# Decayed attention, routed experts and a Mish layer: attention scores on two row halves, updates by heads, counting one step later, and six experts taken in falling order of their counts

## The chip, the core and the metric

The program runs on one core of a Trainium2 chip. Its engines are TensorE (PE; PEld is its weight load), VectorE (DVE), ScalarE (ACT), GpSimd (POOL) and SyncE (SP), each with a queue of its own that it works through in order; DMA queues move data between the device memory and the two on-chip memories, SBUF and PSUM. The metric is device time in microseconds; smaller is better.

## What is computed

Three stages, one behind the other, all in float32. Attention with a decay by blocks (2 batches, 8 heads, 768 rows, 64 per head); a layer of 8 experts, where each of the 1536 rows goes to the one expert of its largest logit; and a dense layer with a Mish curve.

```
for b in range(nb):                                   # blocks of the sequence
    intra = einsum('bhic,bhjc->bhij', qb, kb) * Dmask    # lam ** (i - j), lower triangle
    intra = einsum('bhij,bhjd->bhid', intra, vb)
    inter = einsum('bhid,bhde->bhie', qb * lam_pow, kv_state)
    out[:, :, sl] = intra + inter
    kv_state = lam_block * kv_state + einsum('bhsd,bhse->bhde', kb * rev_pow, vb)

expert_idx = argmax(x @ w_gate)                       # experts
for e in range(E):
    mask = expert_idx == e
    out[mask] = gate_w[mask, None] * (maximum(x[mask] @ w1[e], 0) @ w2[e])

h = x @ w_in                                          # dense layer
return (h * tanh(log1p(exp(h)))) @ w_out
```

## The kernel before

Attention runs in 12 steps, `STEPS`: 6 chunks of 128 rows for each of 2 batches, in turn. Step i first asks for the tiles of step i + 2 (`load_step`: k_t, q, v_n, k_n; three buffers each, all on SP's queue). Then `scores(i + 1)` multiplies keys and queries; q lies in the tile `qbd`, 2 x 64 rows with zeros in the other half, so that one matmul of 256 columns (line 393) gives both heads of a pair. VectorE multiplies the scores by the decay table `dec` (line 397). `factors(i + 1)` runs on GpSimd: `kd` (line 409), then `qs` in two operations, the sum of the two halves of `qbd` (line 415) and the product with the powers `pw` (line 416). `rows(i - 1)` turns the finished rows and forms the logits (line 474); `pick(i - 1)` finds the largest on VectorE, and its one-hot row goes to `oh_all` (line 501). `values(i)` adds state times q (line 433) and scores times v (line 442, in column halves) in PSUM, and then forms the update `u` of the state (line 451, four matmuls of which half is used). `place(i - 1)`, the counting, comes next: two small matmuls (lines 510 and 511) give each row its slot in its expert's bin, VectorE adds the one-hot rows to `obs` (line 526) and writes `slot_i` (line 527), ScalarE scales the rows by their gate (lines 517 and 521), and GpSimd scatters them to the bins in device memory (line 533). `update(i)` ends the step (line 465). In steps 1 to 8 a piece of expert weights (128 x 1024) is loaded and split in two f32r parts: the high part on ScalarE (line 189), the low part on VectorE one step later (line 194).

The experts' stage takes expert after expert in 4 chunks each, `g` of 32, always with a window of `WIN` = 232 columns. `up(g)` (line 719) has 24 f32r matmuls of 232 columns; `down(g - 1)` (lines 740 and 743) has eight of 464 columns and eight of 232. The weights come in 64 pieces, in the order of the experts; `advance(2 * g + 7)` splits them three chunks ahead. `tables()` works out, on VectorE and before the first chunk, where each expert's rows begin in the result (`off_i`) and which rows lie outside the window. `pad(e)` writes zero rows behind each bin from GpSimd's queue, and `load_x(e)` fetches a bin on SP's queue. The dense layer follows in 48 chunks. At the very end a branch (line 882) runs a slow loop for rows outside the windows, if there are any.

The code is written in the order in which it runs; each engine takes its instructions in that order, and a wait holds everything behind it on the same engine.

Of the kernel before, what the change touches and what calls it, by code (L numbers as in the profile page):

```python
# [11 lines left out]
F32 = mybir.dt.float32  # L12
# [27 lines left out]
REST = WIN - P  # L40
FF = 2048
# [5 lines left out]
NX = -(-NT // WIN) - 1  # L47
# [13 lines left out]
def kernel(  # L61
# [52 lines left out]
    cmax = const.tile([P, NE], F32, name="cmax")  # L114
# [5 lines left out]
    eps = const.tile([P, 1], F32, name="eps")  # L120
# [44 lines left out]
    with tc.manual_schedule():  # L165
# [9 lines left out]

        def load_piece():
# [93 lines left out]
        with ExitStack() as actx:  # L270
            ap = actx.enter_context(pool("attn"))

            qbd = []
            for i in range(3):
                t = ap.tile([P, 2, NP, P], F32, name=f"qbd{i}")
                qbd.append(t)
            DVE.memset(qbd[0][HD:P, 0], 0.0)
            DVE.memset(qbd[0][0:HD, 1], 0.0)
            for t in qbd[1:]:
                POOL.memset(t[0:HD, 1], 0.0)  # L280
                POOL.memset(t[HD:P, 0], 0.0)

# [41 lines left out]

            dec = ap.tile([P, NH, P], F32, name="dec")
            pw = ap.tile([P, NP, P], F32, name="pw")
# [4 lines left out]
            def decay(g):  # L331
                h = slice(4 * g, 4 * g + 4)
                DVE.tensor_copy(out=sc0[:, h, :], in_=lam_b[:, h].unsqueeze(2).to_broadcast([P, 4, P]))
# [5 lines left out]
            def powers():  # L339
                DVE.tensor_copy(out=sc0[:, 0:NP, :], in_=lam_p.unsqueeze(2).to_broadcast([P, NP, P]))  # L340
# [19 lines left out]
            POOL.memset(eps, 1e-9)  # L360
# [5 lines left out]
            def constants():  # L366
                for i, (n, b) in enumerate(STEPS):
                    POOL.iota(tok[:, i:i + 1], pattern=[[0, 1]], base=b * SEQ + n * P, channel_multiplier=1)
                POOL.iota(
                    steps, pattern=[[WIN, NX]], base=WIN, channel_multiplier=0, allow_small_or_imprecise_dtypes=True)  # L370
# [3 lines left out]
                POOL.memset(ones8, 1.0)  # L374
                POOL.memset(zeros, 0.0)
# [3 lines left out]
            pt, qs, kd, xt, sld, rk, us, direct = {}, {}, {}, {}, {}, {}, {}, {}  # L379
            NS = len(STEPS)  # L380

            def scores(i):
# [4 lines left out]
                for g in range(2):  # L387
                    if i == 0:
                        decay(g)
                    a = ps.tile([P, 2, 2 * P], F32, tag="a", name=f"a{i}_{g}", bufs=3)  # L390
                    for j in range(2):
                        hp = 2 * g + j
                        PE.matmul(
                            out=a[:, j, :].rearrange("p (a i) -> p a i", a=2), lhsT=k_t[:, hp, :], rhs=q[:, :, hp, :],
                            start=True, stop=True)
                    t = ap.tile([P, 4, P], F32, tag="pt", name=f"pt{i}_{g}", bufs=4)
                    DVE.tensor_tensor(
                        out=t.rearrange("p h i -> p (h i)"), in0=a.rearrange("p h i -> p (h i)"),
                        in1=dec[:, 4 * g:4 * g + 4, :].rearrange("p h i -> p (h i)"), op=ALU.mult)
                    pt[i, g] = t  # L400

            def factors(i):
# [4 lines left out]
                if n < NCH - 1:  # L407
# [3 lines left out]
                        in1=dec[:, :, P - 1:P].to_broadcast([P, NH, HD]), op=ALU.mult)  # L411
# [15 lines left out]
            def values(i):  # L427
# [10 lines left out]
                for h in range(NH):  # L438
                    if h == NH // 2 and i == NS - 2:
                        place(i - 1)  # L440
# [566 lines left out]
```

## Time and profile before

| | us |
|---|---|
| median of 3 runs | 542.11 (541.70 to 542.39) |
| the profiled execution | 541.75 |
| its span, first to last instruction | 540.1 |
| TensorE busy | 522.6 (97%) |
| VectorE busy | 369.8 (68%) |
| ScalarE busy | 324.7 (60%) |
| GpSimd busy | 185.2 (34%) |

By the trace attention lasts up to about 87 us, the experts up to about 269 us, and the dense layer to the end. The shares are means over the three stages, whose limits differ. An f32 matmul appears as two records in the trace, an f32r or bf16 matmul as one. The duration of a matmul record reaches into the next one; the distance of their starts tells the pace.

### The profile page before, as it was taken

Reading aid. Unit: us, or ns where it says so; the run is one execution under the profiler, and the core shown is the slowest. Engines: PE = TensorE matmul, PEld = TensorE weight load, DVE = VectorE, ACT = ScalarE, POOL = GpSimd, SP = SyncE. Lnnn points to the kernel's source line nnn. Section 1 sums busy time; section 2 is a strip of 40 time slices with the busy share of each in tenths; the row PEclk is TensorE's granted clock in tenths of the full one; section 3 lists DMA queues with packets and bytes.
Section 4 is the critical chain, followed back from the end, with each engine's and each line's share of the span. In section 5 each row is a group of like instructions: output and inputs, shape, how many; then the busy total and the mean of one; then the engine's idle time right before and its main releaser. Section 6 shows DMA issues by size and latency. Waiting matters only on the chain. (4 is left out here: it accounts for less than half of the span.)

```text
span 540.1 us, 8441 instructions
## 1 busy us (share of the span) xinstructions
PE 522.6 (97%) x3101; PEld 451.4 (84%) x3102; DVE 369.8 (68%) x668; ACT 324.7 (60%) x514; POOL 185.2 (34%) x151
## 2 busy tenths in 40 slices
PE   8999988999999999999999999999999999999993
PEld 5888878999999999999788878888888888888882
DVE  7999965765967858653498776567965778436362
ACT  1566533655674566555678876777666775765650
POOL 7788842755573331235100321003210031103032
PEclk9999999999999999999999999999999999999997
DMA  8999837119999996731301024020230000001022
GB/s 259 340 329 332 277 147 292 52 49 399 315 299 224 223 360 236 262 128 40 118 0 62 18 79 133 23 79 0 95 139 4 0 0 1 0 1 58 21 80 81
DMA packets 28944, 74.98 MB, mean 139 GB/s; under 512 B 6652, under 2 KB 6652, under 8 KB 28896
## 3 DMA queue, kind: packets, MB, share of 16 engines
q1 hardware_dynamic: 25040, 66.62, 38.3%
q0 software_dynamic: 3424, 7.23, 3.6%
q8 instruction: 26, 0.43, 0.4%
q10 hardware_dynamic: 432, 0.53, 0.3%
q14 instruction: 22, 0.18, 0.1%
HBM read 66.61 MB, written 10.49 MB: 143 GB/s over the span
## 5 line engine op out<-in xcount | busy, mean ns | idle before, releaser
L194 POOL TENSOR_TENSOR lo_f<-w,hi_f 128x1024 fp32r<-128x1024 f32 x16 | 39.8, 2487 | 185.9 <-ACT hi_f L189 155.1
L719 PE MATMUL h<-x,hi_w 128*128 128x232 f32 x512 | 87.5, 274 | 0.0
L740 PE MATMUL y<-hh,hi_w 128*128 128x464 f32 x256 | 84.8, 380 | 0.9 <-DVE hh L723 0.9
L796 PE MATMUL hp<-yt,hi_f 128*128 128x512 f32 x256 | 79.3, 391 | 0.0
L719 PEld LDWEIGHTS h<-x,hi_w 128*128 128x128 f32 x512 | 77.8, 192 | 0.0
L828 PE MATMUL acc<-hi_f,ghi 128*128 128x512 f32 x192 | 76.2, 397 | 0.4 <-ACT Y L833 0.4
L828 PE MATMUL acc<-hi_f,glo 128*128 128x512 f32 x192 | 75.8, 395 | 0.0
L828 PE MATMUL acc<-lo_f,ghi 128*128 128x512 f32 x192 | 75.7, 394 | 0.0
L136 DVE TENSOR_TENSOR t<-t,hp 128x512 f32<-128x512 f32 x48 | 32.8, 684 | 61.1 <-ACT t L135 61.1
L719 PE MATMUL h<-x,lo_w 128*128 128x232 f32 x256 | 71.1, 278 | 0.0
L743 PE MATMUL y<-hh,lo_w 128*128 128x232 f32 x256 | 69.1, 270 | 0.0
L194 DVE TENSOR_TENSOR lo_w<-raw,hi_w 128x1024 fp32r<-128x1024 f32 x50 | 63.0, 1283 | 7.5 <-ACT hi_w L189 6.9
L132 ACT ACTIVATE t<-hp 128x512 f32<-128x512 f32 x48 | 28.6, 600 | 62.4 <-PE hp L796 62.1
L189 ACT ACTIVATE hi_w<-raw 128x1024 fp32r<-128x1024 f32 x64 | 64.5, 1055 | 0.9 <-DMA raw<-in_w1p_dram 0.9
L194 POOL TENSOR_TENSOR lo_w<-raw,hi_w 128x1024 fp32r<-128x1024 f32 x14 | 35.1, 2510 | 71.5 <-ACT hi_w L189 70.8
L796 PEld LDWEIGHTS hp<-yt,hi_f 128*128 128x128 f32 x256 | 48.1, 188 | 11.1
L740 PEld LDWEIGHTS y<-hh,hi_w 128*128 128x128 f32 x256 | 48.2, 188 | 6.1 <-DVE hh L723 1.1
L796 PE MATMUL hp<-yt,lo_f 128*128 128x512 f32 x128 | 50.4, 394 | 0.0
L719 PEld LDWEIGHTS h<-x,lo_w 128*128 128x128 f32 x256 | 49.0, 191 | 0.5
L743 PEld LDWEIGHTS y<-hh,lo_w 128*128 128x128 f32 x256 | 48.9, 191 | 0.0
L722 ACT ACTIVATE hh<-h 128x464 fp32r<-128x464 f32 x32 | 17.8, 558 | 49.7 <-PE h L719 45.2
L723 DVE SCALAR_TENSOR_TENSOR hh<-h,hh 128x464 fp32r<-128x464 f32 x32 | 20.4, 639 | 34.8 <-ACT hh L722 34.8
(163 smaller groups left out, 1032.9 us busy)
## 6 DMA issues: line engine op xcount, KB each, us to landing
raw<-in_w1p_dram SPq DMA_DIRECT2D x32, 512.0 KB
raw<-in_w2p_dram SPq DMA_DIRECT2D x32, 512.0 KB
w<-in_w3p_dram SPq DMA_DIRECT2D x32, 512.0 KB
xw<-bins SPq DMA_DIRECT2D x7, 512.0 KB
qbd<-in_qT_dram SPq DMA_DIRECT2D x24, 128.0 KB
v_n<-in_vN_dram SPq DMA_DIRECT2D x12, 256.0 KB
k_n<-in_kN_dram SPq DMA_DIRECT2D x10, 256.0 KB
k_t<-in_kT_dram SPq DMA_DIRECT2D x10, 256.0 KB
```

The costliest lines, as they stand in the source:

```text
L132: yield lambda: ACT.activation(out=t, in_=h, func=AF.Tanh, scale=0.5)
L136: yield lambda: DVE.tensor_tensor(out=t, in0=t, in1=h, op=ALU.mult)
L189: ACT.activation(out=hi, in_=r, func=AF.Copy)
L194: engine.tensor_tensor(out=lo, in0=r, in1=hi.bitcast(F32), op=ALU.subtract)
L719: PE.matmul(out=p[:, m, :], lhsT=w[:, s], rhs=x[k // 2][:, k % 2, r, :], start=(k == 0 and m == 0 and z == 0), stop=(k == KD - 1 and z == ...
L722: ACT.activation(out=h[:, :, 0, :], in_=p, func=AF.Relu)
L723: DVE.scalar_tensor_tensor(out=h[:, :, 1, :], in0=p, scalar=0.0, in1=h[:, :, 0, :].bitcast(F32), op0=ALU.max, op1=ALU.subtract)
L740: PE.matmul(out=y.rearrange("p z n -> p (z n)"), lhsT=whi[:, s], rhs=h[:, f].rearrange("p z n -> p (z n)"), start=(c == 0 and f == 0), sto ...
L743: PE.matmul(out=y[:, 1, :], lhsT=wlo[:, s], rhs=h[:, f, 0, :], start=False, stop=(c == 3 and f == 1), skip_group_check=True)
L796: PE.matmul(out=p, lhsT=w[:, s], rhs=x, start=(k == 0 and z == 0), stop=(k == KD - 1 and z == 2))
L828: PE.matmul(out=acc[t], lhsT=x[:, s], rhs=w[:, DM:2 * DM], start=(first and z == 0), stop=(last and z == 2))
```

## The change

Attention. q is loaded as it is, without zeros (one transfer a step in place of two), and the scores are eight matmuls a step on the two halves of the rows, 64 each, that write two PSUM tiles by turns; `dec` is ordered by halves accordingly. `qs` is one operation on GpSimd. The update `u` is eight matmuls by heads, 64 by 64 each. `place` is cut into `weigh`, `locate` and `scatter`: the gate's scaling stays in the step, the counting and the scatter of a row tile come one step later. The negated maximum and the sum for the gate move from VectorE to ScalarE. The split of weight pieces begins in step 3 and not in step 1; 16 pieces are loaded before the experts' stage and not 19.

Experts. Experts 0 and 1 keep their places and 232 columns. The six others are sorted by falling count on the chip; place by place they get windows of 232, 212, 200, 192, 180 and 168 columns. Their weights and rows are fetched by an index that SP reads from the table `who_i`. The loop at the end takes what lies outside the windows in pieces of 128 rows.

```diff
+WINS = (WIN, WIN, 232, 212, 200, 192, 180, 168)
+NSORT = 6
+OWIN = P
...
+        def expert(e):
+            if e not in experts:
+                j = e - (NE - NSORT)
+                experts[e] = SP.value_load(who_i[0:1, j:j + 1], min_val=0, max_val=NE - 1)
+            return experts[e]
...
-            SP.dma_start(out=r, in_=(w1p, w2p)[s][e, c])
+            w = (w1p, w2p)[s]
+            if e < NE - NSORT:
+                SP.dma_start(out=r, in_=w[e, c])
+            else:
+                SP.dma_start(out=r, in_=w[ds(expert(e), 1), c].rearrange("o p f -> p (o f)"))
...
-                q = qbd[i % 3]
+                q = ap.tile([P, NP, P], F32, tag="q", name=f"q{i}", bufs=3)
...
-                SP.dma_start(out=q[0:HD, 0], in_=qT[i, 0:HD])
-                SP.dma_start(out=q[HD:P, 1], in_=qT[i, HD:P])
+                SP.dma_start(out=q, in_=qT[i])
...
+                a = [ps.tile([P, NP, P], F32, tag="a", name=f"a{i}_{z}", bufs=3) for z in range(2)]
+                for hp in range(NP):
+                    for z in range(2):
+                        r = slice(z * HD, (z + 1) * HD)
+                        PE.matmul(out=a[z][:, hp, :], lhsT=k_t[r, hp, :], rhs=q[r, hp, :], start=True, stop=True)
...
-                    POOL.tensor_tensor(out=s, in0=q[:, 0], in1=q[:, 1], op=ALU.add)
-                    POOL.tensor_tensor(out=s, in0=s, in1=pw, op=ALU.mult)
+                    POOL.tensor_tensor(out=s, in0=q, in1=pw, op=ALU.mult)
...
-                    for hp in range(NP):
+                    for h in range(NH):
+                        hp, z = divmod(h, 2)
                         PE.matmul(
-                            out=u[:, hp, :], lhsT=kd[i][:, 2 * hp:2 * hp + 2, :].rearrange("p h d -> p (h d)"),
-                            rhs=v_n[:, hp * P:(hp + 1) * P], start=True, stop=True)
-                if 1 <= i < NS - 2:
-                    place(i - 1)
+                            out=u[z * HD:(z + 1) * HD, hp, :], lhsT=kd[i][:, h, :],
+                            rhs=v_n[:, h * HD:(h + 1) * HD], start=True, stop=True)
...
-                DVE.tensor_scalar(out=nm, in0=m8[:, 0:1], scalar1=-1.0, scalar2=None, op0=ALU.mult)
+                ACT.activation(out=nm, in_=m8[:, 0:1], func=AF.Copy, scale=-1.0)
...
                 scores(i + 1)
+                if 2 <= i < NS - 1:
+                    locate(i - 2)
...
                 factors(i + 1)
+                if 2 <= i < NS - 1:
+                    scatter(i - 2)
...
+                if 1 <= i < NS - 1:
+                    weigh(i - 1)
                 values(i)
...
-                if 1 <= i <= 8:
+                if 3 <= i <= 8:
                     p, r = next_raw()
...
-            for _ in range(5):
+            for _ in range(2):
                 load_piece()
...
         def tables():
...
+            DVE.tensor_tensor(
+                out=above, in0=key[:, n0:NE].unsqueeze(1).to_broadcast([P, NSORT, NSORT]),
+                in1=key[:, n0:NE].unsqueeze(2).to_broadcast([P, NSORT, NSORT]), op=ALU.is_gt)
+            DVE.tensor_reduce(out=rank, in_=above, axis=AX.X, op=ALU.add)
...
+            by_place(who_f, iota8[:, n0:NE])
+            DVE.tensor_copy(out=who_i, in_=who_f)
...
-        with tc.If(flag > WIN):
+        with tc.If(flag > 0):
```

TensorE, one step of attention, before. `a` are the scores, `r` the turned rows with the logits, `o` the values, `u` the update, `c` the counts:

```order
L393 MATMUL a_0_611<-qbd_107,k_t_514 128x256 x2
L393 MATMUL a_1_616<-qbd_107,k_t_514 128x256 x2
L474 MATMUL r_0_631<-rw,xt_575 128x136 x3
L474 MATMUL r_1_632<-rw,xt_575 128x136
L433 MATMUL o_651<-qs_534,state_160 128x128 x4
L442 MATMUL o_651<-pt_0_525,v_n_427 64x128 x4
L442 MATMUL o_651<-pt_1_530,v_n_427 64x128 x4
L451 MATMUL u_666<-v_n_427,kd_532 128x128 x4
L510 LDWEIGHTS tri
L510 MATMUL c_671<-obs,tri 128x8
L511 LDWEIGHTS tri
L511 MATMUL c_671<-oh_all,tri 128x8
```

The same engine after, from the update of one step to the state of the next:

```order
L471 MATMUL u_428<-v_n_196,kd_298 64x64 x8
L414 MATMUL a_0_447<-q_349,k_t_350 128x128
L414 MATMUL a_1_448<-q_349,k_t_350 128x128
...
L540 LDWEIGHTS tri
L540 MATMUL c_461<-obs,tri 128x8
L541 LDWEIGHTS tri
L541 MATMUL c_461<-oh_all,tri 128x8
L492 MATMUL r_0_478<-rw,xt_426 128x136 x3
L492 MATMUL r_1_479<-rw,xt_426 128x136
L454 MATMUL o_503<-qs_380,state_163 128x128 x4
```

The count matmuls stood behind the update of their step; now they stand behind the scores, one step later. The two score tiles alternate, and the update has smaller matmuls.

GpSimd, one step of attention, before (`bins` is the scatter):

```order
L533 DMA bins<-xs_588,slot_i 12288x512
L409 TENSOR_TENSOR kd_621<-k_n_520,dec 128x512
L415 TENSOR_TENSOR qs_623<-qbd_107 128x512
L416 TENSOR_TENSOR qs_623<-qs_623,pw 128x512
L533 DMA bins<-xs_677,slot_i 12288x512
```

And after:

```order
L555 DMA bins<-xs_500,slot_i 12288x512
L431 TENSOR_TENSOR kd_661<-k_n_540,last 128x512
L437 TENSOR_TENSOR qs_663<-q_534,pw 128x512
L555 DMA bins<-xs_596,slot_i 12288x512
L431 TENSOR_TENSOR kd_759<-k_n_638,last 128x512
```

One operation in four is gone; the order of the others is the same, but the scatter belongs to an earlier step.

SP at the start of the experts' stage, after (`xw` are an expert's rows, `raw` its weight pieces):

```order
L760 DMA xw_1323<-bins 128x2x512
L195 TENSOR_LOAD who_i
L195 ISA x2
L208 ISA
L208 DMA raw_1670<-in_w1p_dram 128x1024
L208 ISA
L208 DMA raw_1685<-in_w2p_dram 128x1024
L762 ISA
L762 DMA xw_1691<-bins 128x2x512
L208 ISA
L208 DMA raw_1741<-in_w1p_dram 128x1024
```

Before, three more pieces stood ahead of the first of these `xw` loads and none between the first and the second; now two stand between them, behind the read of `who_i`.

## Rows read from the trace of the kernel before

**Rows 1.** Stretches (us): length, busy time by engine, PEclk, DMA share, GB/s

```profile
12.00:31.00 19.00, 18.10 (x154) 16.34 (x153) 17.86 (x53) 9.25 (x24) 16.12 (x32) 1.00 1.04 340
31.00:69.00 38.00, 36.74 (x297) 30.91 (x296) 35.91 (x108) 23.18 (x60) 32.16 (x24) 1.00 0.97 311
69.00:87.00 18.00, 15.44 (x125) 13.40 (x124) 11.52 (x57) 5.68 (x17) 7.10 (x8) 1.00 0.57 214
87.00:178.00 91.00, 90.09 (x695) 87.06 (x694) 62.18 (x88) 51.25 (x75) 51.64 (x33) 1.00 0.71 228
```

**Rows 2.** Timeline of PE in attention: start, duration, line, output<-inputs, records

```profile
18.63 1.97 PE L393 MATMUL a<-qbd,k_t 128*128 128x256 f32 x8
...
24.41 1.97 PE L393 MATMUL a<-qbd,k_t 128*128 128x256 f32 x8
...
43.22 1.97 PE L393 MATMUL a<-qbd,k_t 128*128 128x256 f32 x8
45.18 1.19 PE L474 MATMUL r<-rw,xt 128*128 128x136 f32 x8
46.21 1.05 PE L433 MATMUL o<-qs,state 128*128 128x128 f32 x8
47.20 1.09 PE L442 MATMUL o<-pt,v_n 128*64 128x128 f32 x16
48.22 1.16 PE L451 MATMUL u<-v_n,kd 128*128 128x128 f32 x8
49.22 0.17 PE L510 MATMUL c<-obs,tri 128*128 128x8 bf16 x1
49.60 0.17 PE L511 MATMUL c<-oh_all,tri 128*128 128x8 bf16 x1 [0.21 <-DVE oh_all L501]
```

**Rows 3.** Timeline of POOL in the same step, and of a later one

```profile
43.10 2.21 POOL L416 TENSOR_TENSOR qs<-qs,pw 128x512 f32<-128x512 f32 x1
46.18 1.01 POOL L533 DMA_INDIRECT bins<-xs,slot_i  x1 [0.86 <-DVE state L465]
47.22 1.06 POOL L409 TENSOR_TENSOR kd<-k_n,dec 128x512 f32<-128x512 f32 x1
48.23 1.27 POOL L415 TENSOR_TENSOR qs<-qbd 128x512 f32<-128x512 f32 x1
...
68.02 1.27 POOL L416 TENSOR_TENSOR qs<-qs,pw 128x512 f32<-128x512 f32 x1
```

**Rows 4.** Timeline of DVE in the same step

```profile
44.50 0.83 DVE L526 TENSOR_TENSOR obs<-obs,oh_all 128x8 bf16<-128x8 bf16 x1
...
48.42 1.12 DVE L501 TENSOR_SCALAR oh_all<-iota,i 128x8 bf16<-128x8 f32 x1
49.46 1.21 DVE L194 TENSOR_TENSOR lo_w<-raw,hi_w 128x1024 fp32r<-128x1024 f32 x1
```

**Rows 5.** Timeline of PEld: first loads of the values, of the update

```profile
47.19 0.20 PEld L442 LDWEIGHTS o<-pt,v_n 128*64 128x64 f32 x4
...
48.22 0.41 PEld L451 LDWEIGHTS u<-v_n,kd 128*128 128x128 f32 x3 [0.17 <-issue]
```

**Rows 6.** Timeline of PE in the experts' stage: end of an up, begin of a down

```profile
119.48 0.28 PE L719 MATMUL h<-x,lo_w 128*128 128x232 f32 x1
...
120.83 0.38 PE L740 MATMUL y<-hh,hi_w 128*128 128x464 f32 x1
121.04 0.27 PE L743 MATMUL y<-hh,lo_w 128*128 128x232 f32 x1
121.14 0.38 PE L740 MATMUL y<-hh,hi_w 128*128 128x464 f32 x1
```

**Rows 7.** Timeline of PE: the last logits, 8 columns each

```profile
79.44 1.06 PE L482 MATMUL lg<-rw,xt 128*128 128x8 f32 x8 [0.70 <-ACT xt L446]
```

**Rows 8.** Timeline of DVE at the start of the experts' stage

```profile
88.47 0.17 DVE L648 TENSOR_TENSOR_SCAN incl<-ones,base 128x8 f32<-128x8 f32 x1
...
90.66 0.17 DVE L664 TENSOR_TENSOR pos_i<-pos_f,slot_f 128x12 int32<-128x12 f32 x1
92.87 1.19 DVE L723 SCALAR_TENSOR_TENSOR hh<-h,hh 128x464 fp32r<-128x464 f32 x2 [2.04 <-ACT hh L722]
```

More of the change, by code (lines that the diff above doesn't have):

```diff
@@ L46 @@
 UNITS = 33
-NX = -(-NT // WIN) - 1
+NX = -(-(NT - min(WINS)) // OWIN)
 NPIECE = NE * 8
@@ L113 @@
     first_i = const.tile([P, NE, NX], I32, name="first_i")
-    cmax = const.tile([P, NE], F32, name="cmax")
+    key = const.tile([P, NE], F32, name="key")
+    above = const.tile([P, NSORT, NSORT], F32, name="above")
+    rank = const.tile([P, NSORT], F32, name="rank")
+    sel = const.tile([P, NSORT, NSORT], F32, name="sel")
+    part = const.tile([P, NSORT, NSORT], F32, name="part")
+    count = const.tile([P, NE], F32, name="count")
+    who_f = const.tile([P, NSORT], F32, name="who_f")
+    who_i = const.tile([P, NSORT], I32, name="who_i")
+    at_f = const.tile([P, NE], F32, name="at_f")
+    wins = const.tile([P, NE], F32, name="wins")
+    thr = const.tile([P, NE], F32, name="thr")
+    over_f = const.tile([P, NE, NX], F32, name="over_f")
+    cmax = const.tile([P, 8], F32, name="cmax")
     cmax_i = const.tile([P, 1], I32, name="cmax_i")
@@ L174 @@
         n_load, n_split = [0], [0]
+        experts = {}
+        def expert(e):
[3 more added lines that the diff above has]
+            return experts[e]
         def load_piece():
@@ L325 @@
             dec = ap.tile([P, NH, P], F32, name="dec")
+            lam_z = lam_b.rearrange("p (h z) -> p z h", z=2)
+            last = ap.tile([P, NH], F32, name="last")
             pw = ap.tile([P, NP, P], F32, name="pw")
@@ L374, in constants @@
                 POOL.memset(ones8, 1.0)
+                for j, w in enumerate(WINS):
+                    POOL.memset(wins[:, j:j + 1], float(w - OWIN))
                 POOL.memset(zeros, 0.0)
@@ L443, in values @@
                         out=o[z * HD:(z + 1) * HD, hp, :], lhsT=v_n[:, h * HD:(h + 1) * HD],
[L444 removed]
+                        rhs=pt[i, z][:, hp, :], start=(n == 0 and hp == 0), stop=True, skip_group_check=True)
                 x = ap.tile([P, NP, P], F32, tag="xt", name=f"xt{i}", bufs=2)
@@ L521, in place, with locate @@
                     ACT.activation(out=xs[:, n:NP], in_=rv[1], func=AF.Copy, scale=gt[:, 0:1])
+            def locate(i):
+                c = ps.tile([P, NE], F32, tag="c", name=f"c{i}", bufs=1)
+                PE.matmul(out=c, lhsT=tri[:, 1, :], rhs=obs, start=True, stop=False)
+                PE.matmul(out=c, lhsT=tri[:, 0, :], rhs=oh_all[:, i, :], start=False, stop=True)
                 jk = ap.tile([P, NE], F32, tag="jk", name=f"jk{i}", bufs=1)
@@ L531, in place, with scatter @@
                         out=hot, in0=iotaw, scalar1=slot_f[:, i:i + 1], scalar2=None, op0=ALU.is_equal)
-                    direct[i] = (xs, hot)
+                    direct[i] = (xg[i], hot)
+            def scatter(i):
                 POOL.indirect_dma_start(
                     out=bin_views[i], out_offset=IOA(ap=slot_i[:, i:i + 1], axis=0),
-                    in_=xs.rearrange("p a c -> p (a c)"), in_offset=None)
+                    in_=xg.pop(i).rearrange("p a c -> p (a c)"), in_offset=None)
+            def place(i):
+                weigh(i)
+                locate(i)
+                scatter(i)
             def spread(i, g, start):
@@ L569 @@
                 late = []
+                if 1 <= i < NS - 1:
+                    weigh(i - 1)
                 values(i)
+                if i == NS - 2:
+                    locate(i - 1)
+                    scatter(i - 1)
                 if i == 0:
@@ L578 @@
                 if i in (9, 10):
-                    for _ in range(2):
+                    for _ in range(3):
                         load_piece()
@@ L736, in down @@
                 for m in range(KD):
-                    y = ys[e][m]
+                    y = ys[e][m][:, :, 0:w]
                     for f in range(2):
                         s = slice(f * DM + m * P, f * DM + (m + 1) * P)
-                        PE.matmul(out=y.rearrange("p z n -> p (z n)"), lhsT=whi[:, s],
-                                  rhs=h[:, f].rearrange("p z n -> p (z n)"), start=(c == 0 and f == 0), stop=False,
+                        PE.matmul(out=y, lhsT=whi[:, s], rhs=h[:, f], start=(c == 0 and f == 0), stop=False,
                                   skip_group_check=True)
@@ L912, in overflow @@
             DVE.tensor_copy(out=xt[:, 2 * g:2 * g + 2, :], in_=p)
-        h = op.tile([P, NE, WIN], F32, name="o_h")
-        y = [ps.tile([P, 2, WIN], F32, tag=f"y{i}", name=f"o_y{i}", bufs=1) for i in range(2)]
+        h = op.tile([P, NE, OWIN], F32, name="o_h")
+        y = [ps.tile([P, 2, OWIN], F32, tag=f"y{i}", name=f"o_y{i}", bufs=1) for i in range(2)]
         for c in range(4):
```

158 lines of the change are left out of this document (84 added, 74 removed).

## The prediction

> **What bounds the kernel now.** I read the stages first [rows 1]. In the experts' stage TensorE works 90.09 of 91 us, so a saving there counts in full, but only if it shortens what TensorE itself does. In attention it also looks full (36.74 of 38 us), yet three others are as full: VectorE 35.91, GpSimd 32.16, and the DMA engines at a share of 0.97 while they move 311 GB/s (1.04 at 340 GB/s in the stretch before). The granted clock is 1.00, the 2.4 GHz level, in all of them; I expect no change of it.
>
> Then one attention step on TensorE [rows 2]. From the scores at 43.22 to the count matmul at 49.60, plus its 0.10, a step is 6.48 us: scores 1.96, r 1.03, state times q 0.99, values o 1.02, update u 1.00, counting 0.48. In the last row TensorE waits 0.21 for the one-hot rows. Steps without the load of a split are shorter: 5.78 from 18.63 to 24.41. An f32 matmul stands as two records: eight records of 256 columns in 1.96 are 0.24 each.
>
> What sets 6.48 is a ring between GpSimd and VectorE. GpSimd's rows fill it [rows 3]: wait 0.86, scatter 1.01, kd 1.06, sum of the q halves 1.27, product with pw 2.21, and small gaps. The scatter needs slot_i, which stands behind the update of obs; that tiny bf16 operation takes 0.83 and ends at 45.33, as GpSimd's product (43.10 before it, 2.21 long) ends at 45.31 [rows 3, 4]. In the same way the one-hot operation takes 1.12 and ends at 49.54, as the sum of the halves ends at 49.50. So two VectorE operations on eight columns, a size that costs 0.17 elsewhere [rows 8], wait for GpSimd to finish, and GpSimd waits for the first of them. The product takes 1.27 where no weight split runs on VectorE (68.02) and 2.21 where one does (49.46, 1.21 long).
>
> **The change part by part.**
>
> *Plain q, scores on row halves.* Removed: GpSimd's sum of the halves (1.27 and 0.09 of gap in each step), the zeroing of the q tiles, one DMA per step. The four score matmuls of 256 columns become eight of 128 columns on 64 rows, in pairs on the two halves. No row of before shows row halves. Column halves do exist there: the values o are 16 records of 128 columns in 1.02, where u needs 1.00 for eight [rows 2], so the two halves run side by side. Their weight loads do too: four loads of 64 columns lie within 0.20, where three of 128 columns lie within 0.41, that is 0.19 and twice 0.11 [rows 5]; four in a row at half of 0.11 would reach 0.30. I take row halves to behave as column halves: eight pairs of records at 0.112, 0.90. The other end is no overlap, 16 times 0.112, 1.79.
>
> *Change of tiling.* The three groups from 46.21 to 49.22 hold two changes and take 3.01 (u's 1.00 included), where 24 slots of 0.111 are 2.66: 0.17 for a change. Before there are two in a step, after there are three (u to scores, scores to count, state to values): 0.52.
>
> *Update by heads.* Four matmuls of 128 by 128 become eight of 64 weight columns and 64 moving columns, in the tiling of the values. Pairs at half of 0.112 give 0.45; if a pair can't go under 0.112, 0.90. I take 0.55, near the low end, since the loads of [rows 5] came at that pace.
>
> *TensorE's new step*: 0.90 + 0.55 + 0.52 + r 0.93 + state 0.90 + o 0.87 + count 0.05 = 4.7; at the bad ends 6.0.
>
> *Counting a step back.* The count matmuls move behind the scores of the next step, so the 0.21 goes. The wait is put on VectorE instead: the reciprocal now follows three ScalarE operations in a row (negated maximum, exponential, weight), with the state update and the next masks queued behind it. With a weight split ahead of it (1.21) that is covered; without one I count 0.5, in steps that VectorE doesn't bound. The scatter moves on GpSimd's queue too, from behind values to behind the factors, and its rows leave one step later.
>
> *The ring after.* GpSimd keeps 6.48 - 1.36 = 5.1; with the product at 1.27, 4.2. VectorE, full today, loses its two small operations (0.3) and up to 1.5 of waiting: 4.7. DMA: a step moves four tiles of 0.26 MB, a weight piece of 0.52 and a scatter of 0.26, 1.83 MB; at 340 GB/s 5.4, at 311 5.9, and q as one transfer over all partitions may be quicker. So the next limit is DMA, hardly above the others. I take 5.4 for the six steps with a split (two fewer pieces are split here than before): six times 1.1, 6.5. The three before them go from 5.8 to 5.0 (4.7 and some of the 0.5), 2.5. The start, without zeroing, gives 0.5. For the last two steps, where TensorE idles 2.56 of 18 [rows 1], I take a step's 1.1 and 0.9 from the shorter product. **Attention: 11.5**, between 3.5 and 15.
>
> *Windows of 232 to 168 columns.* The experts lose 20, 32, 40, 52 and 64 columns, 208 in all. Up: twelve records of 232 columns take 120.83 - 119.48 = 1.35, 0.112 each [rows 6]. Eight records of only 8 columns, with the same 128-column weights, take 1.06 [rows 7]; if the last lasts 0.28 as in [rows 6], they start 0.111 apart. So it is the weight load that sets the pace of up, and fewer columns give nothing there. The Trainium skill, "TensorE: Matmul & The Clock Gate", section Back-to-back issue gap, gives N/2.4 + 2.5 ns for a lone matmul; by that, up would shrink with the columns; the trace has 112 where it gives 99. Down: a pair is one matmul of two times 232 columns, 0.21, and one of 232, 0.10 [rows 6]. The second can't fall (a weight load must fit in it); the first falls by 0.21/464 = 0.453 ns a column, 32 times an expert: 32 x 2 x 208 x 0.453 = **6.0**. Bounds 5.5 and 7.
>
> *Sorting.* Tables on VectorE: 13 operations in 2.36 (88.47 to 90.83) become 23 [rows 8]. At 0.18 each they end at 92.65, just before hh is taken up at 92.87, after an idle 2.04 that hides them; at 0.25 they would cost 1.4. I take 0. The rest (what is left over) goes to chunk 26, beside TensorE's work. SP must read the expert's number before pieces 16 on; these loads queue ahead of and behind the rows of expert 2, whose wait is there already. They are three chunks ahead of their use; uncovered, a piece of 0.52 MB costs 1.5 at 340 GB/s, and two could be late: 3.
>
> **Sum.** The profiled execution took 541.75 (span 540.1), 0.36 under the median 542.11. 541.75 - 11.5 - 6.0 = 524.25; against the median 524.6. **Forecast 524.5**, alone from 518 to 530.
>
> **Rivals.**
> *Weight loads of the two row halves go one after another.* Then scores keep 1.79, TensorE's step is 5.6 to 6.0, attention gives 3.5 to 8, and the time is 528 to 532.5; I put 530. For it: the load is as long for 64 rows if it goes by columns. Against: [rows 5]. The Trainium skill, same page, section LDWEIGHTS, has a load go by columns and not by rows, which alone would give this rival; its section Part 3 lets loads overlap in different row groups, which gives the forecast. No run here shows row halves. DMA at 311 GB/s instead of 340 would end at the same place (6 x 0.5 less).
> *Up does shrink with the columns.* 128 x 208 x 0.453 ns = 12 more, 512. Against it [rows 7].
> *Overflow (slower).* If one sorted expert has more rows than its window, the loop at the end runs. From the reference's inputs I get 195 and 205 for the first two and 227, 205, 194, 185, 168, 157 in falling order, under 232, 232 and 232, 212, 200, 192, 180, 168: margins of 5 to 12 rows. One count over decides; the price is at least the reload of the weights, 8 expert pieces and 32 of the dense layer at 0.52 MB, 21 MB, 62 us at 340 GB/s, so 585 or more.
> *The work is moved but a new wait eats it*: late pieces (3), tables (1.4), the gather that opens the experts' stage (2): 524.6 + 6.4 = 531, inside the range.
>
> **How the numbers follow.** Forecast 0.66, serial loads or slower DMA 0.18, new waits 0.06, shorter up 0.04, overflow 0.06. From 517 to 533 lie the forecast with its own bounds, the serial loads and the new waits, 0.90 less their tails; the unknown ends of u, of the tilings and of DMA lie in it too, so I keep it at that. Differences under 0.2% can't be told from none. Faster 0.92, same 0.02, slower 0.06.
>
> **What would show it.** A pair of scores at 0.11, not 0.22; eight-record u at 0.5; steps near 5.4 with a split; obs no longer ending with a GpSimd operation; up still at 0.112 for expert 7, down's first matmul at 0.15; hh of chunk 0 not later than before. Wrong if scores stay at 1.8, if up shortens, or if the end of the program shows the loop.

## The result and the profile after

The changed kernel takes **533.15 us** (median of four runs, 532.8 to 534.09) against 542.03 for the kernel before (541.7 to 542.39): ratio 0.9828, 95% interval 0.9804 to 0.9851. It is faster, as forecast, but by 8.9 us where 17.5 were forecast, and the time lies at the very edge of the range: 0.15 us above its upper end of 533 in microseconds, just inside it as a ratio (533 of the 542.11 that the prediction started from is 0.9832).

The span of the profiled execution falls by 8.0 us, from 540.08 to 532.08. This execution of the changed kernel is the slowest of its four (534.09 us) and has the lowest mean granted clock (0.979; the others 0.985 to 0.991), so the stretches below show a little more loss than the median has. Five marks on TensorE's timeline (start, duration, then line and operation) divide it: the scores of steps 5 and 11, the experts' first up, the first down and the dense layer's first matmul. First the kernel before:

```profile
30.25 0.45 PE L393 MATMUL a<-qbd,k_t 128*128 128x256 f32 x1
...
69.47 0.46 PE L393 MATMUL a<-qbd,k_t 128*128 128x256 f32 x1
...
86.93 0.43 PE L719 MATMUL h<-x,lo_w 128*128 128x232 f32 x1
...
93.57 0.48 PE L740 MATMUL y<-hh,hi_w 128*128 128x464 f32 x1 [0.91 <-DVE hh L723]
...
262.53 0.41 PE L796 MATMUL hp<-yhi,lo_f 128*128 128x512 f32 x1
```

Then the changed kernel:

```profile
29.23 0.38 PE L414 MATMUL a<-q,k_t 64*128 64x128 f32 x2
...
62.40 0.38 PE L414 MATMUL a<-q,k_t 64*128 64x128 f32 x2
...
81.87 0.44 PE L795 MATMUL h<-x,lo_w 128*128 128x232 f32 x1
...
89.04 0.48 PE L817 MATMUL y<-hh,hi_w 128*128 128x464 f32 x1 [1.45 <-DVE hh L799]
...
255.06 0.47 PE L874 MATMUL hp<-yhi,lo_f 128*128 128x512 f32 x1
```

| stretch | before | after | change | forecast |
|---|---|---|---|---|
| start to the scores of step 5 | 30.25 | 29.23 | -1.0 | -3.0 |
| six steps with a weight split | 39.22 | 33.17 | -6.05 | -6.5 |
| scores of step 11 to the first up | 17.46 | 19.47 | +2.0 | -2.0 |
| first up to first down | 6.64 | 7.17 | +0.5 | 0 |
| first down to the dense layer | 168.96 | 166.02 | -2.9 | -6.0 |
| dense layer to the end | 277.55 | 277.02 | -0.5 | 0 |

The middle of attention came as forecast. What is missing stands in three places: the start (2.0), the end of attention (4.0) and the experts (3.1).

The first two have the same look. In the stretches of the changed kernel (bounds, length, busy time of PE, PEld, DVE, ACT and POOL, granted clock, DMA share, GB/s) the granted clock, 1.00 in every one of [rows 1], halves twice, from the 2.4 GHz level to the 1.2 GHz level:

```profile
4.00:8.00 4.00, 2.63 (x23) 1.45 (x22) 2.63 (x5) 0.00 (x0) 0.62 (x2) 1.00 1.02 355
8.00:13.00 5.00, 4.23 (x32) 3.20 (x34) 4.60 (x12) 0.60 (x1) 1.34 (x2) 0.53 1.01 354
13.00:18.00 5.00, 5.00 (x40) 4.44 (x40) 4.09 (x6) 0.00 (x0) 4.93 (x31) 0.50 0.77 243
18.00:23.00 5.00, 4.97 (x67) 4.63 (x66) 3.73 (x17) 3.28 (x11) 2.27 (x2) 0.94 0.45 158
68.00:73.00 5.00, 4.07 (x41) 3.42 (x39) 1.15 (x7) 2.24 (x8) 0.96 (x1) 1.00 0.57 225
73.00:80.00 7.00, 6.23 (x21) 5.57 (x22) 2.43 (x16) 1.24 (x5) 1.92 (x2) 0.51 0.69 262
```

Before each fall TensorE had waited. Its timeline ahead of them (the bracket is the idle time and what ended it):

```profile
4.83 1.18 PE L414 MATMUL a<-q,k_t 64*128 64x128 f32 x16
7.35 2.15 PE L414 MATMUL a<-q,k_t 64*128 64x128 f32 x16 [1.34 <-DMA k_t<-in_kT_dram]
...
71.36 1.06 PE L500 MATMUL lg<-rw,xt 128*128 128x8 f32 x8 [0.87 <-ACT xt L465]
...
73.77 1.88 PE L567 MATMUL win_u<-hots,xs 128*128 128x232 f32 x4 [0.83 <-DVE m L514]
```

The first row is the new score matmul at full clock: sixteen records in 1.18. The same sixteen take 2.15 at 7.35, mostly at half clock, and the four records of 232 columns at 73.77 take 1.88. The kernel before has the two waits at the end too, 0.70 [rows 7] and this one, and kept its clock:

```profile
81.85 1.02 PE L540 MATMUL win_u<-hots,xs 128*128 128x232 f32 x4 [0.83 <-DVE m L496]
```

In the experts, the second products did shrink. Expert 7 on TensorE, the row of [rows 6] and what follows it:

```profile
247.82 0.35 PE L817 MATMUL y<-hh,hi_w 128*128 128x336 f32 x1
248.00 0.24 PE L819 MATMUL y<-hh,lo_w 128*128 128x168 f32 x1
248.08 0.27 PE L795 MATMUL h<-x,lo_w 128*128 128x168 f32 x1
248.19 0.38 PE L795 MATMUL h<-x,hi_w 128*128 128x168 f32 x2
248.41 0.28 PE L795 MATMUL h<-x,lo_w 128*128 128x168 f32 x1
```

From start to start the pair of a down takes 0.26 (248.08 less 247.82) where it took 0.31 [rows 6]; three records of up still take 0.33 (248.41 less 248.08), 0.11 each. But the four transposes that turn an expert's rows (L776) start later one from the other than before. From the first of them to the next up at 184.22 they take 0.87, where a group with a second half of 72 rows takes 0.32. PEld's rows for expert 5, whose second half has 64 rows, show the form:

```profile
183.26 0.14 PEld L776 LDWEIGHTS t<-ident,xw 128*128 128x128 f32 x1
183.55 0.60 PEld L776 LDWEIGHTS t<-ident,xw 64*128 64x128 f32 x3 [0.15 <-issue]
184.22 0.19 PEld L795 LDWEIGHTS h<-x,lo_w 128*128 128x128 f32 x1
```

The windows of 192, 180 and 168 columns leave 64, 52 and 40 rows for the second transpose, half of the array's 128 rows or fewer (64*128), in turn with one on all of them.

### The profile page after: what moved, and what is told of

The parts are those of the page before. It is cut to its first block, busy times and chain, and to the rows that moved or that the text cites. A ratio compares the mean times of both kernels' runs of the same rounds, so it can differ in the third digit from the quotient of the medians.

```text
span 532.1 us, 8878 instructions
## 1 busy us (share of the span) xinstructions
PE 512.0 (96%) x3277; PEld 445.4 (84%) x3278; DVE 355.3 (67%) x660; ACT 326.4 (61%) x538; POOL 163.4 (31%) x144
## 5 line engine op out<-in xcount | busy, mean ns | idle before, releaser
L795 PE MATMUL h<-x,hi_w 128*128 128x232 f32 (+5 forms) x512 | 87.4, 274 | 0.0
L817 PE MATMUL y<-hh,hi_w 128*128 128x464 f32 (+5 forms) x256 | 79.4, 369 | 1.4 <-DVE hh L799 1.4
L795 PE MATMUL h<-x,lo_w 128*128 128x232 f32 (+5 forms) x256 | 71.0, 277 | 0.0
L220 DVE TENSOR_TENSOR lo_w<-raw,hi_w 128x1024 fp32r<-128x1024 f32 x50 | 60.7, 1238 | 8.5 <-ACT hi_w L215 8.5
L819 PE MATMUL y<-hh,lo_w 128*128 128x232 f32 (+5 forms) x256 | 65.9, 257 | 0.0
L798 ACT ACTIVATE hh<-h 128x464 fp32r<-128x464 f32 (+5 forms) x32 | 16.4, 512 | 45.5 <-PE h L795 43.1
L906 PEld LDWEIGHTS acc<-hi_f,ghi 128*128 128x128 f32 x192 | 36.1, 188 | 9.4 <-ACT Y L911 1.1
```

The costliest lines, as they stand in the source:

```text
L220: engine.tensor_tensor(out=lo, in0=r, in1=hi.bitcast(F32), op=ALU.subtract)
L795: PE.matmul(out=p[:, m, :], lhsT=w[:, s], rhs=x[k // 2][:, k % 2, r, :], start=(k == 0 and m == 0 and z == 0), stop=(k == KD - 1 and z == ...
L798: ACT.activation(out=h[:, :, 0, :], in_=p, func=AF.Relu)
L817: PE.matmul(out=y, lhsT=whi[:, s], rhs=h[:, f], start=(c == 0 and f == 0), stop=False, skip_group_check=True)
L819: PE.matmul(out=y[:, 1, :], lhsT=wlo[:, s], rhs=h[:, f, 0, :], start=False, stop=(c == 3 and f == 1), skip_group_check=True)
L906: PE.matmul(out=acc[t], lhsT=x[:, s], rhs=w[:, DM:2 * DM], start=(first and z == 0), stop=(last and z == 2))
```

## The experiments

All times are medians of four runs (seven for z_pairs). The kernel before took 542.15 us beside the first four kernels, 542.63 beside the next four, 542.35 beside the last four. "Step" is the mean of the five steps between the scores of steps 6 and 11 in the trace, 5.60 in the changed kernel (34.39 to 62.40).

### Where the missing gain went: transposes and clock

**turn72.** The second transpose never has fewer than 72 rows; the copy behind it still takes the window's columns alone.

```diff
...
-                    for a, n in enumerate((P, w - P)):
+                    for a, n in enumerate((P, max(w - P, 72))):
...
```

> The changed kernel with one edit: the second transpose of each pair in the expert stage takes at least 72 rows and columns (more than 64), also where the expert's window leaves only 64, 52 or 40; what is read of it stays the same. Theory: a transpose of 64 rows or fewer runs on half of the array's rows, and each pair of a whole and a half one costs changes of tiling; the four transposes of a group go from 0.85 us back to 0.32 in the six groups of experts 5 to 7, 3.1 us in all: 530.0 us against 533.15 for the changed kernel. Rival: the groups wait there for PSUM or for the tokens' load, not for the tiling: 533.1.

Measured 529.71 us (ratio to before 0.9767, 0.9743 to 0.9792), 3.4 under the changed kernel. From the first down to the dense layer it takes 162.82 instead of 166.02. The group that took 0.87 takes 0.31 (181.28 less 180.97):

```profile
180.97 0.51 PE L776 MATMUL t<-ident,xw 128*128 128x128 f32 x4
181.28 0.34 PE L795 MATMUL h<-x,lo_w 128*128 128x200 f32 x1
```

The theory holds, with its size: summed over all groups, from the first transpose to what follows the last, the transposes take 4.6 us where the changed kernel has 7.7 and the kernel before 4.8.

**busy_start** and **busy_end.** Spare matmuls, whose results nobody reads, fill TensorE's waits: in busy_start seven of 512 columns after the scores of step 0; in busy_end eight of 256 columns ahead of the last routing scores, and eight ahead of the hot rows.

```diff
             scores(0)
+            for _ in range(7):
+                PE.matmul(out=idle, lhsT=warm[:, 0:P], rhs=warm, start=True, stop=True)
...
+            def busy():
+                for _ in range(8):
+                    PE.matmul(out=keep, lhsT=tri[:, 0, :], rhs=tri.rearrange("p a i -> p (a i)"), start=True, stop=True)
+            busy()
             rows(NS - 1)
             place(NS - 2)
+            busy()
             pick(NS - 1)
```

> The changed kernel with one edit: seven matmuls of 512 columns on zeros stand between the scores of steps 0 and 1, where TensorE was idle for 1.34 us waiting for k_t of step 1. Theory: that idle time is what lets the granted clock fall from 1.00 to 0.50 at 8.3 us; kept busy, the clock stays at 1.00 through 18.4 us, and the work that ran there at half speed is done about 3 us sooner: 530 us, granted clock 1.00 in this stretch. Rival 1: the clock falls all the same (the scores on half of the rows are what brings it down): 533, clock 0.50. Rival 2: the clock stays, but loads and VectorE set the first steps: 533 with a clock of 1.00.

> The changed kernel with one edit: eight small bf16 matmuls of 256 columns stand in each of the two waits of TensorE at the end of attention (0.87 us ahead of the last routing scores, 0.83 us ahead of the hot rows). Theory: these two waits let the granted clock fall from 1.00 to 0.50 at 73.4 us until 80.2; kept busy, 6.8 us of nearly continuous TensorE work takes about half: 530 us. Rival: what sets the end there is VectorE's chain of small instructions, and the time stays at 533, whatever the clock.

busy_end measured 531.83 (0.9805, 0.9784 to 0.9827). In its profile the clock stays up at the end, and the hot rows start at 73.97, 0.2 later than in the changed kernel, yet the first up at 79.05, 2.8 sooner:

```profile
73.00:80.00 7.00, 7.00 (x55) 6.41 (x53) 3.58 (x21) 2.35 (x7) 2.92 (x3) 1.00 0.81 300
```

And the hot rows on TensorE's timeline:

```profile
73.97 1.02 PE L567 MATMUL win_u<-hots,xs 128*128 128x232 f32 x4
```

From the hot rows to the first up it takes 5.08, as in the kernel before (81.85 to 86.93), against 8.10. So the clock cost 3.0 us there in the profiled execution. The median gains only 1.3; the mean granted clock of the four runs of the changed kernel goes from 0.979 to 0.991, so not every run loses as much as the profiled one.

That the spare matmuls kept the clock at the end isn't shown by this. Ten profiles, those of the changed kernel and of nine variants, have the two waits unfilled. In five (the changed kernel, turn72, win232, pool_twice, z_major) the clock fell there, for 3.4 us in the four variants; in the other five (busy_start, count_now, pool_count, z_pairs, q_halves) it stayed at 1.00. With the waits filled it stayed in three of three, which could be chance.

busy_start measured 531.41 (0.9804, 0.9777 to 0.9831). The clock no longer falls at 8.3. It falls at 13.1, for 3.4 us instead of 10, after the next wait of TensorE, 1.42 for kd:

```profile
12.82 0.89 PE L471 MATMUL u<-v_n,kd 128*64 128x64 f32 x16 [1.42 <-POOL kd L431]
```

The stretches around it (the third number from the end is the clock):

```profile
6.00:13.00 7.00, 5.03 (x55) 3.29 (x53) 6.49 (x14) 0.60 (x1) 1.38 (x2) 1.00 1.03 356
13.00:17.00 4.00, 4.00 (x40) 3.66 (x38) 3.83 (x5) 0.00 (x0) 4.00 (x31) 0.57 0.83 256
```

The scores of step 5 start at 28.44, 0.8 sooner. The spare matmuls were not free, though: the scores of step 1 start behind the last of them, at 8.23, where with the wait left and a whole q they start at 7.16 to 8.16 (7.35 in the changed kernel). And it isn't shown that they moved the fall or made it shorter. In the profile of pool_count, where nothing is filled and TensorE waits 1.01 for k_t, the clock also falls only at 13.2, until 16.6. In turn72 and win232, whose attention is the changed kernel's, it falls at 7.7 and 7.9 for 3.4 us only, and step 5 starts at 28.18 and 28.14, sooner than here. So the length of a fall changes from one execution to the next with the same code: 10.3 us at the start of the changed kernel's profile, 3.4 in these two, and the difference is worth about 1.1 us at step 5. Nor did this run lose its clock at the end of attention, with the two waits there unfilled: such a wait is often followed by a fall, not always.

**all_three.** turn72, busy_start and busy_end together.

> The three edits together (transposes of at least 72 rows, matmuls on zeros at the start and at the end of attention). If each of the three theories holds and their gains add up: 3.1 + 3 + 3 us under 533.15, so 524, which is what the prediction's sum had. If only the transposes matter: 530.

Measured **528.33** (0.9729, 0.9706 to 0.9752), the fastest kernel here: 4.8 under the changed kernel, about half of the sum expected. The clock fell from 20.2 to 23.7, after a wait of the routing matmuls for the copy of the values (xt), which stands on ScalarE's queue behind the weighting of the rows of the step before:

```profile
20.08 1.15 PE L492 MATMUL r<-rw,xt 128*128 128x136 f32 x4 [1.61 <-ACT xt L465]
```

In turn72 the same wait, as long, was followed by no fall; the clock there is 1.00 from 11.1 to 72.6:

```profile
20.03 1.19 PE L492 MATMUL r<-rw,xt 128*128 128x136 f32 x8 [1.61 <-ACT xt L465]
```

**all_and_weigh.** all_three, with the weighting behind that copy, and six more spare matmuls ahead of the update of step 0.

```diff
+                    if i == 0:
+                        for _ in range(6):
+                            PE.matmul(out=idle, lhsT=warm[:, 0:P], rhs=warm, start=True, stop=True)
                     for h in range(NH):
...
-                if 1 <= i < NS - 1:
-                    weigh(i - 1)
                 values(i)
+                if 1 <= i < NS - 1:
+                    weigh(i - 1)
```

> The three edits of all_three, and two more: the weighted rows (ScalarE) stand behind the copy of the step's values instead of ahead of it, and six more matmuls on zeros fill TensorE's wait for kd in step 0. Theory: in all_three TensorE waited 1.6 us at 18.5 us for that copy, which stood behind the weighting on ScalarE, and then lost its clock from 20.4 to 23.7; without it the scores of step 4 start at 22.5 instead of 25.2, and later steps lose some of their waits on the copy: 525.5 us. Rival: the PSUM tiles of r come free later, as the weighting reads them, and the next r waits instead: 528.

Measured 528.77 (0.9749, 0.973 to 0.9769): nothing gained over all_three in the median (the span of the profiled execution is 1.0 less, 526.29 against 527.26). Attention does get faster. In its profile the clock is 1.00 from 5.5 to 78.22, step 5 starts at 27.92 and step 11 at 59.83, 1.3 and 2.6 before the changed kernel, and the hot rows 3.0 before it. There TensorE's list of waits from 4 to 79 us (total, times, longest) has a new entry:

```profile
PE a L414 <- DMA q<-in_qT_dram: 2.8, 2, 1.7
PE win_u L577 <- DMA first<-bins: 2.1, 1, 2.1
PE r L495 <- ACT xs L535: 1.3, 2, 0.8
```

The gather of the first expert's rows out of DRAM waits for the scattered rows, so 2.1 us is given back there; the prediction had priced this gather at 2 among its new waits. In the experts' stage TensorE waits another 0.9 for an expert's rows (xw out of the bins). The rival's wait (r for xs) is seen too, with 1.3.

**win232.** All eight windows 232 again.

```diff
-WINS = (WIN, WIN, 232, 212, 200, 192, 180, 168)
+WINS = (WIN,) * 8
```

> The changed kernel with the experts' windows undone: all eight take 232 columns again; the sorting by count and the loads by a register stay. Theory: narrower windows give 5.8 us in the second products and take 3.1 back in the transposes of 64 rows or fewer, so undoing them costs 2.7: 535.9 us against 533.15, with the four transposes of a group at 0.34 us for every expert. Rival: the dear transposes come from the sorting or the loads, not from the windows: 539, with the groups of experts 5 to 7 still at 0.85.

Measured 534.82 (0.9859, 0.9829 to 0.989). First down to dense layer takes 168.96, the kernel before's time and 2.94 more than the changed kernel's; each group of transposes takes 0.34. So the sorting and the loads by a register cost nothing there, and the windows were worth 5.8 in down (its records, from start to start, take 77.4 us in the changed kernel and 83.1 here) and 0.1 in up, less the 3.0 of the transposes.

### What made the steps shorter

**count_now, pool_twice** and **pool_count.** The place of the counting put back; GpSimd's product issued twice; both.

```diff
-                if 2 <= i < NS - 1:
-                    locate(i - 2)
...
-                if 2 <= i < NS - 1:
-                    scatter(i - 2)
...
-                if i == NS - 2:
+                if 1 <= i < NS - 1:
                     locate(i - 1)
                     scatter(i - 1)
...
                     POOL.tensor_tensor(out=s, in0=q, in1=pw, op=ALU.mult)
+                    POOL.tensor_tensor(out=s, in0=q, in1=pw, op=ALU.mult)
```

> The changed kernel with the counting put back: each step counts and scatters the tokens of the step before it (not of two before), behind its own values, as before the change. Theory (the prediction's): the chain of counts between GpSimd and VectorE set the steps at 6.48 us, and the counting a step back is what opened it, so the steps with a piece to split (the five from 34.4 to 62.4 us, 5.60 us each) go back to about 6.3: 537 us. Rival: the shorter work of GpSimd and TensorE, or the loads, made the steps shorter, and the place of the count gives nothing: steps of 5.6, 533.

> The changed kernel with GpSimd's product for q's decay (1.26 us) issued twice in every step, which is what the sum of the halves, removed by the change, used to take. Theory: GpSimd's work is part of the ring with VectorE that sets a step, so the five steps from 34.4 to 62.4 go from 5.60 to 6.2 or more, 3 to 6 us over the loop: 537. Rival: the loads set these steps, and GpSimd has room: under 1 us, 533.5.

> The changed kernel with both relievers of the ring undone at once: the count in its old place and GpSimd's product for q issued twice; TensorE's shorter work (4.80 us in a step) stays. Theory A (the prediction's): the ring of GpSimd and VectorE set 6.48 us before, and either relief alone was enough to open it, so with both undone the five steps with a split go from 5.60 to 6.2 or more. Theory B: before, TensorE itself set the step (6.27 busy of 6.48), and the ring follows it: the five steps stay at 5.6 to 6.0, little over the 5.79 and 5.81 of the two undone one by one.

count_now: 531.9 us (0.9813, 0.9783 to 0.9844), step 5.79. pool_twice: 534.42 (0.9843, 0.9813 to 0.9872), step 5.81. Each alone is worth 0.2 us in a step, and by these two the ring looked like the wrong theory. In the total count_now is even 1.25 us under the changed kernel, at a mean clock of 0.986 to 0.997 in its four runs against 0.979 to 0.991; so counting a step later, taken alone, earned nothing that can be seen. pool_count: **537.63** (0.9924, 0.9903 to 0.9944), and three of its five steps are those of the kernel before to 0.02 us, 6.47, 6.46 and 6.46. (In the fourth the clock fell, 0.78 over 7.78 us, and the fifth, behind it, takes 4.82.) Two of the three:

```profile
35.67:42.14 6.47, 4.95 (x68) 4.41 (x67) 6.22 (x17) 4.22 (x12) 5.49 (x5) 1.00 1.03 396
42.14:48.60 6.46, 4.95 (x68) 4.41 (x67) 6.21 (x17) 4.22 (x12) 5.49 (x5) 1.00 1.03 400
```

TensorE has work for 4.95 of 6.46 us, and the DMA engines bring 400 GB/s, with no engine waiting for a load in the three steps: neither sets the step. VectorE is busy for 6.21, but 2.24 of that are two operations on eight columns that end with a GpSimd operation. GpSimd and VectorE in it are [rows 3, 4] over again. First GpSimd:

```profile
42.02 2.21 POOL L438 TENSOR_TENSOR qs<-q,pw 128x512 f32<-128x512 f32 x1
45.09 1.01 POOL L556 DMA_INDIRECT bins<-xs,slot_i  x1 [0.86 <-DVE state L484]
```

And VectorE:

```profile
43.18 1.07 DVE L547 TENSOR_TENSOR obs<-obs,oh_all 128x8 bf16<-128x8 bf16 x1
...
47.27 1.17 DVE L520 TENSOR_SCALAR oh_all<-iota,i 128x8 bf16<-128x8 f32 x1
48.36 1.21 DVE L220 TENSOR_TENSOR lo_w<-raw,hi_w 128x1024 fp32r<-128x1024 f32 x1
```

obs ends at 44.25 and GpSimd's product at 44.23, and the one-hot operation ends at 48.44, as GpSimd's first product (47.13, 1.28 long) ends at 48.41. The ring set 6.48; either relief opens it as far as the next limit, which is why one undone alone shows so little.

**z_major** and **z_pairs.** The scores half by half (four matmuls on the upper rows, then four on the lower); the same, with the update again in four matmuls of 128 by 128.

```diff
-                for hp in range(NP):
-                    for z in range(2):
+                for z in range(2):
+                    for hp in range(NP):
```

> The changed kernel with the scores' matmuls in another order: the four of the upper row half, then the four of the lower, so that neighbours use the same rows and none runs beside the next. Theory of the prediction: on alternating halves two matmuls run in the time of one; in this order the sixteen records of a step take twice as long, 1.16 to about 2 us, and as TensorE does not set the steps, the total goes up by no more than 2 us: 533 to 535. Rival: TensorE's work is on the path of every step: 0.8 us for each of eleven, 541.

> The changed kernel with TensorE's two savings undone at once: scores ordered half by half, and the update again in four matmuls of 128 by 128; GpSimd's work and the place of the count stay as changed. TensorE's work in a step goes from 4.80 to about 5.8 us. Theory A (ring): the steps with a split stay near 5.6, or at TensorE's own 5.8, never near 6.48. Theory B (TensorE sets the step where it has the most work): 5.8 to 6.0, TensorE at 97% or more, as it was before; total 535 to 537.

z_major: 535.03 (0.9857, 0.9816 to 0.9898), step 5.56. The sixteen records take 1.68 and not 1.16, so neighbours on the two halves do run side by side, and the step is no longer for it. z_pairs: 536.09 (0.9903, 0.9875 to 0.9932), step 5.83 with TensorE full:

```profile
43.08:48.91 5.83, 5.83 (x60) 5.28 (x59) 5.31 (x15) 4.17 (x12) 3.28 (x3) 1.00 1.03 406
```

Both theories allowed 5.8, so this run alone doesn't choose between them; pool_count does. z_pairs shows that TensorE's savings are worth 0.2 in a step: without them TensorE would have been the next limit.

**q_halves.** q by two transfers of 64 partitions.

```diff
-                SP.dma_start(out=q, in_=qT[i])
+                SP.dma_start(out=q[0:HD], in_=qT[i, 0:HD])
+                SP.dma_start(out=q[HD:P], in_=qT[i, HD:P])
```

> The changed kernel with q loaded by two transfers of 64 partitions each, as before the change, instead of one of 128. Theory: the steps wait for the loads in places (q and k_t, 2.4 us from 34 to 47 us), and two half transfers move at a lower rate, so the DMA engines bring less than the 400 GB/s of that stretch, and the five steps from 34.4 to 62.4 go from 5.60 to 6 or more. Rival: the form of q's transfer is nothing to the rate: 5.6, 533.

Measured 533.22 (0.9835, 0.9796 to 0.9873), step 5.85. Steps 6 to 8 of this kernel (columns as in the stretches above):

```profile
33.40:39.04 5.64, 4.81 (x71) 4.40 (x67) 4.74 (x17) 4.59 (x16) 3.28 (x3) 1.00 1.03 352
39.04:45.55 6.51, 5.12 (x70) 4.65 (x67) 5.72 (x18) 4.45 (x13) 3.27 (x3) 1.00 1.05 353
45.55:50.93 5.38, 5.12 (x66) 4.61 (x67) 4.16 (x14) 3.90 (x12) 2.86 (x3) 1.00 1.05 337
```

The changed kernel:

```profile
34.39:40.67 6.28, 4.87 (x70) 4.42 (x67) 5.33 (x18) 4.95 (x14) 3.28 (x3) 1.00 1.01 386
40.67:46.53 5.86, 4.71 (x66) 4.36 (x67) 4.49 (x13) 3.53 (x11) 3.27 (x3) 1.00 1.04 409
46.53:51.68 5.15, 4.80 (x67) 4.40 (x67) 4.69 (x17) 4.18 (x12) 2.90 (x3) 1.00 1.04 401
```

With the DMA engines as busy (1.03 to 1.05 against 1.01 to 1.04), the halves bring 348 GB/s in the mean of the three where the whole q brings 398. The other profiles bear it out: the kernel before, which has halves, brings 345 and 347 in its two fullest steps, at a share of 1.05, and nine variants with the whole q bring 396 to 413 in their steps at a share of 1.04 or 1.05. The halves cost 0.25 in a step of this profile; in the total it can't be told from none.

## Why the prediction was right and wrong

**What bounded attention: right.** The ring of GpSimd and VectorE set 6.48, and pool_count brings 6.46 back with TensorE at 4.95. TensorE's own 6.27 of busy time before looked like an equal bound; it was close behind, and z_pairs, with most of that work back and the ring open, stands at TensorE's 5.83.

**TensorE's new step, 4.7: right**: 4.71 to 4.87 busy in the three steps shown above. Row halves pair as column halves do (the whole group 1.16 with its tail, where 0.90 was taken for the pace), and the rival of serial weight loads falls.

**Steps of 5.4 with a split: nearly.** 5.60 in five of them, 5.53 in all six. The next limit was the loads, as the sum had it, but not alone: TensorE waits 2.4 us for q at 40.67 and 46.53, and in the same five steps 1.4 for ScalarE's copy xt (0.34 and 1.06). One sign failed: obs still ends with a GpSimd operation in the changed kernel (44.34, the product 44.32). The scatter still comes behind it, but GpSimd then stands idle for 1.73 before its next operation, so this no longer sets the step.

**Start and last steps: wrong.** The step that failed is the sentence on the granted clock: "I expect no change of it". TensorE's work got shorter, its waits for xt and the row maximum did not (0.87 and 0.83, where they were 0.70 and 0.83), one of 1.34 for k_t came up, and in the profiled execution the clock then halved for some 10 and some 7 us. Why it falls behind one such wait and not behind another stays open: in the same profile the waits of 1.29 and 1.15 for q were followed by no fall. At the end the clock took 3.0 of the 4.0 that are missing in this execution; the other 1.0 is a gain taken for the last steps that came only by half (step 11 to the last routing scores: 9.97 before, 8.96 after). Of the 2.0 missing at the start, the length of the fall was about 1.1 (turn72 and win232, with the same attention and a fall of 3.4 us). In all_and_weigh, at a clock of 1.00 from 5.5 on and with the weighting moved, 1.3 came back; 0.7 did not come even there, so the gain taken for the start was too large by about that.

**Windows: the size of down right, the sum wrong.** Down gave 5.8 against 6.0, up next to nothing (0.1), as [rows 7] had it. (The rival of a shorter up counted 128 matmuls of an expert; up has 96 of them, which makes 9 us and not 12.) The term that failed is one that wasn't there: the prediction priced a change of tiling at 0.17 in attention and did not count the changes that windows of 192 and fewer columns bring into the transposes. Six groups took 0.83 to 0.87 instead of 0.34, 3.0 us; turn72 took them away again.

**Tables: the cover was gone.** 23 operations were taken at nothing, since an idle 2.04 ahead of hh would hide them [rows 8], with 1.4 as the end if they were slow. That idle time was itself a wait. In the kernel before, ScalarE's part of hh came late, behind a wait that the profile puts down to a weight piece:

```profile
92.28 1.00 ACT L722 ACTIVATE hh<-h 128x464 fp32r<-128x464 f32 x2 [4.41 <-DMA raw<-in_w1p_dram]
```

In the changed kernel ScalarE has it for chunk 0 at 85.63 (85.07 and 0.56), but VectorE is at its tables until 87.82 and starts its own part at 88.34:

```profile
85.07 0.56 ACT L798 ACTIVATE hh<-h 128x464 fp32r<-128x464 f32 x1 [2.27 <-DVE part L686]
```

And VectorE:

```profile
87.65 0.17 DVE L719 TENSOR_TENSOR pos_i<-pos_f,slot_f 128x12 int32<-128x12 f32 x1
88.34 0.64 DVE L799 SCALAR_TENSOR_TENSOR hh<-h,hh 128x464 fp32r<-128x464 f32 x1 [0.52 <-ACT hh L798]
```

What the last bracket names is ScalarE's part for chunk 1, which this operation doesn't need. So the first down, whose wait went from 0.91 to 1.45, waits for the tables and the 0.52 behind them. What that wait would be without the tables was not tried. The overflow loop did not run, and late loads of pieces did not show.

Of the 9.5 us of span that the sum lacked, 3.1 lie in the experts, all but 0.1 of it in the transposes, and 3.0 are the clock at the end; for both a run showed them gone. The start is 2.0, about 1.1 of it the clock, the last steps 1.0, the first down's wait 0.5 and the six steps 0.45, less the 0.5 that came unasked behind the experts.

## What to carry to other kernels

When TensorE's work is cut ahead of waits that stay, look at the clock of those stretches, in more than one execution: the same code lost more of it in one than in another, and the loss was up to 3.0 us in one place. Spare matmuls in the waits are a cheap trial (0.2 us at the end of attention, 0.1 to 1.1 ahead of step 1), but that they keep the clock is not shown here. A narrower tile is priced at every instruction that its width reaches: the transposes of 64 rows or fewer took back 3.0 us, two thirds of the 4.5 that the narrower windows of their three experts save in down (an estimate: 64 x 156 columns at 0.453 ns). Two reliefs of one ring can each look worthless when undone alone: undo both before dropping the theory.

## What the runs showed of the hardware

- Granted clock: during or after waits of 0.8 to 2.4 us in stretches where TensorE otherwise works, it fell to 0.50 (the 1.2 GHz level), for 3.4 to 13.6 us (the longest in z_major, 8.2 to 21.8), in the profiles of the changed kernel and of all its variants but one. Such waits also passed without a fall: 0.70 and 0.83 in the kernel before (78.74 to 81.85), 1.29 and 1.15 in the changed kernel (40.67, 46.53), 1.61 in turn72 (20.03), 2.1 in all_and_weigh, whose clock is 1.00 from 5.5 to 78.22.
- Transposes that alternate 128 rows with 64 or fewer start 0.18 to 0.26 apart, four in 0.83 to 0.87; four whose second half has 72 rows or more take 0.31 to 0.34.
- Two transfers of 64 partitions for q, a quarter of the bytes of a step's own tiles, lower the rate of saturated DMA engines from 398 to 348 GB/s (shares of 1.01 to 1.05 in both).
